# A third place for the half spectrum of a pair in a spectral mixer's forward transform

## The chip, the cores and the metric

One core of one Trainium2 chip runs the whole program. The metric is the device time of one execution in microseconds, as the median of several runs; next to it stands one execution that was taken by the hardware profiler.

## What is computed

The reference is one block of a conditioned network, forward and backward (grad_out comes in, the output and nine gradients go out). Cut to what matters here:

```python
def _A_ref(x, w_r, w_i):                       # S = 2048, D = 1024
    X = jnp.fft.rfft2(x.astype(jnp.float32), axes=(-2, -1))
    X = X * (w_r + 1j * w_i)                   # [2048, 513]
    return jnp.fft.irfft2(X, s=(S, D), axes=(-2, -1)).astype(jnp.bfloat16)

def _B_ref(x, w1, b1, w2, b2):                 # F = 3584
    y = _layernorm(x)
    h = _gelu(y @ w1 + b1)
    return h @ w2 + b2

sa, ca, ga, sb, cb, gb = (silu(c) @ w_mod)     # six rows of 1024
h = _layernorm(x) * (1 + ca) + sa
x = x + ga * _A_ref(h, A_w_r, A_w_i)
h = _layernorm(x) * (1 + cb) + sb
x = x + gb * _B_ref(h, B_w1, B_b1, B_w2, B_b2)
```

The gradients of A_x, A_w_r, A_w_i, B_w1, B_b1, B_w2, B_b2, c and w_mod are computed as well.

## The kernel before, in words

The two-dimensional transform is done with matrix products on folded data. `spectral_core` is called twice: with `fwd=True` for the forward pass and with `fwd=False` for the gradient. Its stages are:

- `s_fwd` transforms along the 2048 tokens, in four classes of rows (CE, SE, CO, SO), with matmuls `pu` that land in the tiles `U`.
- `pair(n, par, m)`, for n = 0 to 7, transforms along the features (matmuls `pcs`, line 505) and casts the results into `cs` (two buffers, `css[n % 2]`). From `cs`, VectorE builds the half spectrum of a pair of row blocks in the tile `Pt`, by a sum and a difference of 128 x 1028 elements. In the forward pass GpSimd stores `Pt` to DRAM as `d_P[n]` (line 523), where the backward pass will read it. Then VectorE multiplies `Pt` by the two weight planes `ws` (products `qa` and `qb`), adds and subtracts them, and writes two rows of `R`.
- `s_inv` transforms back along the tokens (matmuls `pv`, line 565, from `R` to the tiles `V`). The classes CE and SE are done between pair 5 and pair 6, since they need R of pairs 0 to 3; CO and SO are done after pair 7.
- the last loop transforms back along the features (matmuls `po` into `ct`), and `consume` does what follows.

The tiles of a pair come from `new_pair_temps`. `ws2`, `Pt2` and `qa2` hold two places each, used in turn. `qb2` also has two halves: the forward pass uses half 0 for the product `qb`, for every pair, and only the backward pass uses half 1 (product `m2`). The weights of pair n + 1 are fetched by `pair_load`: one plain DMA from SP and one gather from GpSimd for each of the two planes (lines 490 and 491).

Beside the forward transform, TensorE has filler work: `ph_part` (matmuls `pp`, line 684) multiplies the gradient by B_w2 and is laid out over the whole stretch. Later come the two layers of the mixer (lines 802 and 851), their gradients (948, 1071, 1252), and the backward transform with gradient matmuls as filler.

The program is written as a data flow of tiles. A scheduler lays out each engine's order ahead of time, from the dependencies, the order in the text, `tc.high_priority()` (for the casts that empty PSUM) and `tc.issue_after()`; `nc.any` lets it choose the engine of a cast. It also sets the waits: an instruction that writes a buffer waits for those that still read it, DMAs included. Each engine then runs its instructions strictly in the order laid out, and so does GpSimd with the DMAs that it issues.

VectorE's tensor operations go through the helper `tt`, so that the profile shows them all at line 173, and they are told apart by their tiles.

## Time and profile before

| | |
|---|---|
| median of 3 runs | 1469.18 us (1469.07 to 1473.41) |
| the profiled execution | 1474.63 us |
| its span, from the first to the last instruction | 1472.8 us |
| TensorE busy | 1395.1 us, 95% of the span |
| VectorE busy | 1072.9 us, 73% |
| ScalarE busy | 717.8 us, 49% |
| GpSimd busy | 376.5 us, 26% |
| mean granted TensorE clock | 0.988 |
| HBM traffic | 186 GB/s over the span |
| forward pairs, from the first to the last Pt row | 157.6 to 213.8 us |

A time in a row of the profile is the start in us from the first instruction of the span, then the duration. What stands in brackets at the end of a row of the timeline is the idle time of that engine just before it, and what ended it. A row `out<-in` names the tile written and the tiles read; `x8` counts instructions. A row of the waits has the total in us, how often, and the longest. DMA transfers are not rows of the timeline; a row of POOL or SP with DMA in its name is the instruction that issues the transfer.

### The profile page before, as it was taken

The page shows a single profiled execution, that of the slowest core. Times are in us where ns is not written, and L with a number is a line of the kernel's source. Part 1 is how long each engine was busy: PE and PEld are TensorE (multiplying, and loading weights), DVE is VectorE, ACT ScalarE, POOL GpSimd, SP SyncE. Part 2 cuts the span into 40 slices and gives each one's busy share as a digit, 9 for nine tenths or more (in the row PEclk, how much of TensorE's full clock was granted, in tenths as well). Part 3 has the DMA queues.
Part 4 walks back from the last instruction along what each step waited for, and adds up shares of the span by engine and source line. Part 5 has one row for each costly group of instructions (what it writes and reads, how often), then busy time and mean ns, then how long its engine had stood idle before and what let it go on. Part 6 is the DMA issues. An engine that isn't in the chain of part 4 may idle for free. (4 is left out here: it accounts for less than half of the span.)

```text
span 1472.8 us, 18265 instructions
## 1 busy us (share of the span) xinstructions
PE 1395.1 (95%) x6703; PEld 650.6 (44%) x6835; DVE 1072.9 (73%) x1581; ACT 717.8 (49%) x953; POOL 376.5 (26%) x441
## 2 busy tenths in 40 slices
PE   5889989999999999999989999999999999999997
PEld 2434545444444444444434444444444444444443
DVE  5984786898799788887520789888467578898542
ACT  4765545857887666665312333342622434444211
POOL 5720541211112222122211011021245431322422
PEclk9999999999999999999999999999999999999999
DMA  9982563999777776796999275396699998766993
GB/s 335 279 228 58 144 219 114 262 258 335 242 245 232 235 248 223 229 292 216 235 303 250 91 256 186 121 266 172 184 226 242 236 218 220 191 193 181 291 235 115
DMA packets 358366, 324.27 MB, mean 220 GB/s; under 512 B 209386, under 2 KB 301056, under 8 KB 358022
## 3 DMA queue, kind: packets, MB, share of 16 engines
q1 hardware_dynamic: 324166, 207.71, 52.9%
q0 software_dynamic: 34112, 115.41, 22.8%
q8 instruction: 53, 0.87, 0.2%
q14 instruction: 35, 0.29, 0.1%
HBM read 162.06 MB, written 111.20 MB: 186 GB/s over the span
## 5 line engine op out<-in xcount | busy, mean ns | idle before, releaser
L684 PE MATMUL pp<-gBoT,wt 128*128 128x512 bf16 x878 | 196.8, 381 | 5.8 <-DMA wt<-in_B_w_dram 3.2
L948 PE MATMUL pg<-w1T,gzr 128*128 128x512 bf16 x876 | 194.6, 379 | 1.6 <-ACT gn3a L956 0.2
L1252 PE MATMUL gw1acc<-gzh,n3n 128*128 128x512 bf16 x876 | 193.8, 379 | 2.3 <-DMA gzh<-d_gz 1.3
L802 PEld LDWEIGHTS <-w 128*128 128x128 bf16 x896 | 87.6, 98 | 112.5 <-issue 9.0
L684 PEld LDWEIGHTS <-wt 128*128 128x128 bf16 x896 | 87.7, 98 | 109.9 <-issue 4.2
L948 PEld LDWEIGHTS <-gzr 128*128 128x128 bf16 x896 | 86.8, 98 | 107.9 <-issue 4.9
L1252 PEld LDWEIGHTS <-n3n 128*128 128x128 bf16 x896 | 87.5, 98 | 106.1 <-issue 2.8
L802 PE MATMUL pz<-n3Ta,w 128*128 128x512 bf16 x437 | 99.4, 383 | 6.1 <-ACT gt L805 4.1
L1071 PE MATMUL gw2acc<-gB,hhsA 128*128 128x512 bf16 x438 | 99.3, 384 | 3.7 <-ACT gwo L1078 3.1
L802 PE MATMUL pz<-n3Tb,w 128*128 128x512 bf16 x439 | 98.4, 379 | 0.5
L851 PEld LDWEIGHTS <-hhA 128*128 128x128 bf16 x608 | 59.4, 98 | 77.5 <-issue 8.0
L811 ACT ACTIVATE gt<-gt 128x2048 bf16<-128x2048 bf16 x28 | 53.5, 1911 | 71.1 <-DVE gt L173 71.1
L805 ACT ACTIVATE gt<-pz,b_col 128x512 bf16<-128x512 f32 x112 | 72.8, 684 | 28.9 <-PE pz L802 26.9
L173 DVE TENSOR_TENSOR gt<-gt,gt 128x2048 bf16<-128x2048 bf16 x56 | 68.5, 1223 | 21.6 <-ACT gt L813 20.9
L1256 ACT CAST gwo<-gw1acc 128x512 bf16<-128x512 f32 x50 | 29.0, 584 | 113.0 <-PE gw1acc L1252 98.7
L1078 ACT CAST gwo<-gw2acc 128x512 bf16<-128x512 f32 x46 | 26.8, 584 | 111.7 <-PE gw2acc L1071 84.0
L173 DVE TENSOR_TENSOR ct<-ct 128x2048 bf16<-128x2048 bf16 x64 | 75.9, 1217 | 2.6 <-DMA d_n<-ct 1.8
L992 DVE CUSTOM_DVE_ANT_0 otl<-otl 128x1024 bf16<-128x1024 bf16 x24 | 29.0, 1222 | 57.5 <-DMA otl<-in_w_mod_dram 51.5
L1071 PEld LDWEIGHTS <-hhsA 128*128 128x128 bf16 x448 | 44.1, 99 | 56.4 <-DMA hhsA<-d_hh 3.6
L807 ACT ACTIVATE gt<-gt 128x2048 bf16<-128x2048 bf16 x28 | 53.4, 1908 | 0.6
L813 ACT ACTIVATE gt<-gt 128x2048 bf16<-128x2048 bf16 x28 | 53.4, 1907 | 0.5
L1257 POOL DMA_DIRECT2D out_dram<-gwo x56 | 30.9, 553 | 78.9 <-ACT gwo L1256 46.8
(317 smaller groups left out, 2520.1 us busy)
## 6 DMA issues: line engine op xcount, KB each, us to landing
gzr<-d_gz SPq DMA_DIRECT2D x28, 512.0 KB
wblk<-in_w_mod_dram SPq DMA_DIRECT2D x12, 1024.0 KB
out_dram<-otl POOLq DMA_DIRECT2D x48, 256.0 KB
out_dram<-gwo POOLq DMA_DIRECT2D x96, 128.0 KB
d_ph<-pho POOLq DMA_DIRECT2D x21, 512.0 KB
d_hh<-hhA POOLq DMA_DIRECT2D x19, 512.0 KB
w2sD<-in_B_w_dram SPq DMA_DIRECT2D x14, 512.0 KB
hhC<-d_ph SPq DMA_DIRECT2D x14, 512.0 KB
```

The source lines that it names most:

```text
L173: return nc.vector.tensor_tensor(out=out, in0=a, in1=b, op=op)
L684: last_pe[0] = nc.tensor.matmul(pp[:], lhsT=wt[:, fg % 2, cch, k * P:(k + 1) * P], rhs=gBoT[j][:, cch, :], start=(cch == 0), stop=(cch == ...
L802: last_pe[0] = nc.tensor.matmul(pz[:], lhsT=w1s[g][:, cch, k * P:(k + 1) * P], rhs=n3T[:, cch, :], start=(cch == 0), stop=(cch == NDC - 1))
L805: nc.scalar.activation(out=zb[:, k, :], in_=pz[:], func=ACT.Identity, bias=b1_col[:, fc:fc + 1], scale=1.0)
L807: nc.scalar.activation(out=av, in_=zb, func=ACT.Square)
L811: nc.scalar.activation(out=sg, in_=bv, func=ACT.Sigmoid, scale=2.0 * GK)
L813: nc.scalar.activation(out=bv, in_=bv, func=ACT.Sigmoid, scale=-2.0 * GK)
L851: last_pe[0] = nc.tensor.matmul(pbs[i][:], lhsT=hh[:, k, i * P:(i + 1) * P], rhs=wp[:, k, :], start=False, stop=(g == 6 and k == 3))
L948: last_pg[0] = nc.tensor.matmul(pgs[i][:], lhsT=gzs[b, g][:, k, i * P:(i + 1) * P], rhs=w1Ts[g][:, k, h * KH:(h + 1) * KH], start=(g == 0 ...
L1071: nc.tensor.matmul(acc[:], lhsT=hh_of(fc)[:, t, :], rhs=gBs[t // 4][:, t % 4, h * KH:(h + 1) * KH], start=(t == 0), stop=(t == NT - 1))
L1252: nc.tensor.matmul(acc[:], lhsT=n3ns[t // 4][:, t % 4, cch * P:(cch + 1) * P], rhs=gz2[t // 8][:, t % 8, :], start=(t == 0), stop=(t == NT ...
L1257: nc.gpsimd.dma_start(out=out_4[cch * P:(cch + 1) * P, fg * 512:(fg + 1) * 512], in_=ob)
```

## The change

In the forward pass the place of `Pt` now goes round three instead of two. Pairs 0, 3 and 6 use place 0 of `Pt2`, pairs 1, 4 and 7 place 1, and pairs 2 and 5 use half 1 of `qb2`, seen in the shape of a place of `Pt2`. The backward pass keeps its two places. Nothing else is touched: the stores to `d_P`, the products and their order in the text are the same.

```diff
@@ pair, in spectral_core @@
-            Pt = Pt2[:, n % 2]
+            Pt = qb2[:, 1].rearrange("p a b w -> p (a b) w") if fwd and n % 3 == 2 else Pt2[:, n % 3 if fwd else n % 2]
             cv = cs.rearrange("p t (x w) -> p t x w", w=PW)
             tt(Pt[:, 2:0:-1, :], cv[:, 0], cv[:, 1], ALU.add)
             tt(Pt[:, 0:4:3, :], cv[:, 0], cv[:, 1], ALU.subtract)
```

## The prediction

> **What bounds the kernel now.** The page comes first. TensorE is busy for 95% of the span, so a change pays only where it fills an idle stretch of TensorE, or where it raises its clock.

> ```profile
> span 1472.8 us, 18265 instructions
> ...
> PE 1395.1 (95%) x6703; PEld 650.6 (44%) x6835; DVE 1072.9 (73%) x1581; ACT 717.8 (49%) x953; POOL 376.5 (26%) x441
> ```

> Next, the view of who waited for whom, between 100 and 420 us, first for TensorE and then for VectorE. The edited lines run here, from 154 to 220 us.

> ```profile
> PE pv L565 <- DVE R L173: 3.9, 1, 3.9
> ...
> DVE Pt L173 <- DMA d_P<-Pt: 2.5, 1, 2.5
> ```

> VectorE waits once for the buffer that the change adds. TensorE waits once for R. The timeline shows that they are one chain:

> ```profile
> 181.31 0.58 POOL L523 DMA_DIRECT2D d_P<-Pt  x1
> ...
> 188.72 0.69 DVE L173 TENSOR_TENSOR Pt<-cs 128x1028 bf16<-128x1028 bf16 x1 [2.47 <-DMA d_P<-Pt]
> ...
> 191.14 1.29 DVE L173 TENSOR_TENSOR R<-qa 128x1026 bf16<-128x1026 bf16 x2
> ...
> 191.89 1.03 PE L565 MATMUL pv<-smi,R 128*128 128x512 bf16 x2 [3.93 <-DVE R L173]
> ...
> 198.89 0.69 DVE L647 CAST V<-pv 128x512 bf16<-128x512 f32 x1 [1.15 <-PE pv L565]
> ```

> Counting the 16 Pt rows from 157.61 us, those at 188.72 and 190.54 are pair 4. Its place is pair 2's, and pair 2's store was issued only at 181.31, because two gathers held GpSimd (rows below). The sums for pair 4 stand in VectorE's order ahead of the last four steps of pair 3 (two on qa, two on R), so R of pair 3 is late. TensorE has used up its filler (pp in the timeline, from 182.94 to 187.95) and stands for 3.94 us. The stretches show what the clock does then (time; PE, PEld, DVE, ACT and POOL busy; granted clock; DMA share, GB/s):

> ```profile
> 191.00:192.00 1.00, 0.11 (x1) 0.11 (x2) 1.00 (x3) 0.68 (x2) 0.48 (x1) 0.88 0.88 353
> 192.00:193.00 1.00, 1.00 (x4) 0.39 (x4) 1.00 (x2) 1.00 (x3) 0.10 (x1) 0.50 0.43 173
> ...
> 195.00:196.00 1.00, 1.00 (x6) 0.40 (x5) 1.00 (x3) 0.56 (x1) 1.00 (x1) 0.91 0.53 134
> ```

> From 191.76 to 195.18, 3.42 us, the clock is half: 1.71 us of work lost.

> **The change part by part.** No instruction is added or removed. Pt of pairs 2 and 5 goes to the idle half of qb2, and the other pairs alternate so that a place is reused after three pairs.

> *Pair 4's wait, removed.* Pair 4 now takes pair 1's place, whose store was issued at 165.24; the longest store seen took 7.41 us from issue (181.31 to 188.72), so it is free by 172.7. The other conditions hold: cs of pair 4 was cast from 172.81 to 174.75. The sum starts at 186.25 behind qb: 2.47 us earlier. R of pair 3 ends at 189.36 instead of 191.83 and TensorE resumes at 189.42: **-2.47 us**.

> *The half clock, removed.* The gap left is 3.94 - 2.47 = 1.47 us. A gap of 2.07 us ahead of 1291.18 leaves the clock at 1.00, so this one should: **-1.71 us**. By then TensorE is 4.18 us ahead.

> *What is late next.* The seventh tile of V is cast by VectorE, between the two R steps of pair 4 (198.89). TensorE would have it ready at 194.65 (198.83 - 4.18) and the next one, in the other PSUM place, 0.86 us later at 195.51. VectorE's first R step ended at 197.74; shifted by 2.47 that is 195.27, and the cast (0.69) frees the place at 195.96, some 0.05 more with the signal. TensorE gives back **+0.50 us**. All that follows hangs on TensorE (cs of pair 6 at 207.18, ct at 234.04, where VectorE had been idle 11.9 us), and moves by the same amount.

> *Reuse of the third place and the others*, **0**: pair 5 wants its place at 192.16, whose store landed at 188.72. Pairs 6 and 7 want theirs after 205; their stores were issued at 186.09 and 191.52, and with 7.41 us are in by 198.9. Cover for pair 5 is 3.4 us; without it the sum would wait for the remainder.

> *Time of the sums and products*, **0**: the places are 4,112 bytes long and lie alike; the same sums take 681 ns in the forward tiles and 688 ns in the backward ones.

> *ws of pair 4*, **0**: its products are wanted at 189.88 and 191.02. GpSimd ended its gathers at 184.26 and 185.51. The one gather that VectorE waited for (pair 3's second, 1.61 us) ended at 181.31 and released qb at 185.01, 3.70 us later; that gives 187.96 and 189.21. The bounds are 0 and 2.47, since at 192.35 nothing was waited for; I take the end nearest to the 3.70 row.

> *ws of pair 5* is what I am least sure of. Its gathers ran in VectorE's pause, which the change closes:

> ```profile
> 169.44 4.75 POOL L491 DMA_INDIRECT ws<-in_A_w_r_dram,xu  x1 [3.63 <-DVE qa L173]
> ...
> 175.08 6.23 POOL L491 DMA_INDIRECT ws<-in_A_w_i_dram,xu  x1 [0.30 <-issue]
> ...
> 186.97 1.02 POOL L491 DMA_INDIRECT ws<-in_A_w_r_dram,xu  x1 [0.30 <-issue]
> ```

> The third had the pause; the first two had two-input work on VectorE with no break, and ended 0.93 us after VectorE turned to a cast from PSUM (173.26, 180.37). Yet those at 161.65 and 163.72, beside the same kind of work, took 1.76 and 1.48. Between a cost of 0 and of 1.6 us (second rival) I take 0, because products of pair 5 come 9 us after the issue.

> [...]

> **Sum:** -2.47 - 1.71 + 0.50 = -3.7 us. The profiled execution took 1474.63 (span 1472.8 and 1.83 around it), so it would be 1470.9. That execution lies 5.45 above the median 1469.18 of the runs; taken off the median, 1465.5, which is 0.25%. The bound of 0.3%, about what a measurement of this kernel can tell from no change, is 4.4 us.

> **The rivals.**

> 1. *Forecast*, 1465.5. Its own spread is the clock's: a gap of 3.08 us (ahead of 1132.86) brought half clock, one of 3.18 (ahead of 333.72) none, so gaps of about 3 us can fall either way once all behind 190 has moved. Each is worth 1.7 us: 1463.8 or 1467.2. Two that cost now can fall away (1132.86, and 1206.20 with 3.43), one can appear; so slightly more than half of this case lies beyond -4.4. Chance 0.49: 0.26 faster, 0.23 within.
> 2. *The gain is taken back by ws of pair 5, or was not there to take.* If the gather of 186.97 is held until the cast at 195.27, it ends at 196.20, the second at 197.5, landing at 201.2; from there pair 5 needs 3.89 us (201.24 to 205.13) and ends at 205.1, when cs of pair 6 is wanted at 203.5. The gain shrinks by 1.6, to 2.1: 1467.1. With pairs 6 and 7 pushed back too, 1469.2. The same 1469.2 comes out if the unprofiled runs had no such wait: two of them lie 4.3 us below the third, about the 4.2 of this wait and its clock. Chance 0.15, within.
> 3. *The order is written anew.* The scheduler lays out every engine's order from the dependencies. Seven more pp matmuls (0.223 each, 22 in 4.91) ahead of the wait for R would close the 1.47 us: 1464.0. All 32 of them behind it would leave TensorE idle from 182.94 to 189.42, 6.5 us instead of 3.9, with the half clock: 1471.7, and more where casts change engines. Against it: pairs 1 to 5 stand in one pattern on VectorE (qb, one sum of the next pair, two steps, the other sum, R), so the store did not shape the order of pair 4. Chance 0.21: 0.11 faster, 0.02 within, 0.08 slower.
> 4. *Slower: the store of the third place holds qb.* The third place lies in the tile that every pair's qb writes. If the tile is guarded whole, qb of pair 2 (176.21) waits for pair 2's store to land: at 180.1 if it is issued as soon as the sums end (172.73 + 7.41), at 188.72 if it stays behind both gathers. The hold is 3.9 to 12.5 us, the middle 8.2. Pair 4's wait is gone but R of pair 3 comes 8.2 - 2.47 = 5.7 later, and TensorE stands for it: 1474.9. It decides from a hold of 6.9 us (2.47 + 4.4). Against it: pair 3 wrote one half of Pt2 at 177.35 while the store of the other half was issued only at 181.31, so halves are guarded apart. Chance 0.15: 0.12 slower, 0.03 within.

> **How the numbers follow.** Faster 0.26 + 0.11 = 0.37; slower 0.08 + 0.12 = 0.20; within 0.23 + 0.15 + 0.02 + 0.03 = 0.43. The likeliest single case has 1465.5, with its own range 1463.8 to 1467.2. The range for 8 in 10 holds it, the second rival, and the inner parts of the third and fourth: 1461 to 1473. Left out are the upper half of the fourth and the ends of the third.

> **What the changed profile would show.** Right: no Pt waiting for d_P; TensorE's wait for R down from 3.9 to about 1.5 us; clock 1.00 throughout 187 to 197; the V cast on VectorE directly behind R. The second rival: a POOL gather near 187 that takes 5 to 9 us, and qa or qb of pair 5 waiting for ws. The third: another number of pp matmuls ahead of pv near 190. The fourth: qb waiting for d_P. The forecast is wrong if the wait for d_P is gone and TensorE's stand near 190 is not shorter.

## The result, and the profile after

| | before | after |
|---|---|---|
| median of the runs | 1471.55 us (22 runs; the first three of them gave the 1469.18 of above) | 1465.61 us (22 runs) |
| lowest and highest | 1466.2 and 1478.5 | 1461.02 and 1470.12 |
| the profiled execution | 1474.63 us | 1469.58 us |
| its span | 1472.8 us | 1467.6 us |
| forward pairs and the first half of `s_inv` (see below) | 79.34 us | 75.32 us |

The ratio is 0.9961, with a 95% interval of 0.9948 to 0.9974: faster by 0.39%, or 5.7 us (3.8 to 7.7). The middle of the interval lies beyond the bound of 0.3%, its lower end (0.26%) just inside.

The page first. The instructions are the same in number, and TensorE's share of the span is as before.

```profile
span 1467.6 us, 18265 instructions
...
PE 1397.0 (95%) x6703; PEld 652.8 (44%) x6835; DVE 1073.8 (73%) x1581; ACT 718.0 (49%) x953; POOL 365.7 (25%) x441
```

Who waited for whom, of TensorE and VectorE, between 150 and 215 us (total, how often, the longest):

```profile
DVE qb L173 <- DMA ws<-in_A_w_i_dram,xu: 1.4, 1, 1.4
...
PE pv L565 <- DVE R L173: 1.1, 1, 1.1
...
PE pv L565 <- ACT V L647: 0.2, 1, 0.2
```

There is no row in which VectorE waits for `d_P`. TensorE's wait for R is down from 3.9 to 1.1 us. The timeline of the same spot, after:

```profile
180.56 0.59 POOL L523 DMA_DIRECT2D d_P<-qb  x1
...
184.04 1.23 DVE L173 TENSOR_TENSOR qb<-Pt,ws 128x2052 bf16<-128x2052 bf16 x1 [1.38 <-DMA ws<-in_A_w_i_dram,xu]
...
185.19 0.69 DVE L173 TENSOR_TENSOR Pt<-cs 128x1028 bf16<-128x1028 bf16 x1
...
187.60 1.29 DVE L173 TENSOR_TENSOR R<-qa 128x1026 bf16<-128x1026 bf16 x2
...
188.35 0.61 PE L565 MATMUL pv<-smi,R 128*128 128x512 bf16 x2 [1.14 <-DVE R L173]
...
193.51 0.69 DVE L173 TENSOR_TENSOR R<-qa 128x1026 bf16<-128x1026 bf16 x1
194.12 0.69 DVE L647 CAST V<-pv 128x512 bf16<-128x512 f32 x1
```

The store of pair 2 now reads `qb` (half 1 of `qb2`) and is issued as late as before, still behind both gathers. But pair 4's sum at 185.19 follows `qb` without a bracket, so it waits for nothing. The clock (time; PE, PEld, DVE, ACT and POOL busy; granted clock; DMA share, GB/s) stays at 1.00 in every microsecond from 186 to 197; three of them:

```profile
187.00:188.00 1.00, 0.21 (x1) 0.00 (x0) 1.00 (x3) 0.23 (x1) 0.70 (x2) 1.00 0.89 283
188.00:189.00 1.00, 0.65 (x4) 0.41 (x5) 1.00 (x3) 1.00 (x3) 1.00 (x1) 1.00 1.02 397
...
191.00:192.00 1.00, 1.00 (x7) 0.41 (x5) 1.00 (x3) 0.72 (x2) 1.00 (x1) 1.00 0.89 247
```

**A measure of the stage.** The 22 runs of before spread over 12 us, so differences of 2 us are read from a stretch of the trace instead: from the first `pcs` matmul of pair 0 to the long row of `po` matmuls behind the last pair. The two rows that begin it and end it, in the timeline of before:

```profile
154.50 5.52 PE L505 MATMUL pcs<-em,U 128*128 128x256 bf16 x48
...
233.84 8.46 PE L630 MATMUL po<-gm,V 128*128 128x256 bf16 x76
```

and of after:

```profile
153.76 5.51 PE L505 MATMUL pcs<-em,U 128*128 128x256 bf16 x48
...
229.08 8.46 PE L630 MATMUL po<-gm,V 128*128 128x256 bf16 x76
```

233.84 - 154.50 = 79.34 and 229.08 - 153.76 = 75.32, so the stage lost 4.02 us. A second profiled execution of the changed kernel (e11 below) gave 75.34. This measure is called "the stage" from here on. One run of e4 below, 1843 us, was slow and is left out of its ratio; all others are fast.

### The profile page after: what moved, and what is told of

Same layout as the page of the kernel before. It is cut to its first block, busy times and chain, and to the rows that moved or that the text cites. A ratio compares the mean times of both kernels' runs of the same rounds, so it can differ in the third digit from the quotient of the medians.

```text
span 1467.6 us, 18265 instructions
## 1 busy us (share of the span) xinstructions
PE 1397.0 (95%) x6703; PEld 652.8 (44%) x6835; DVE 1073.8 (73%) x1581; ACT 718.0 (49%) x953; POOL 365.7 (25%) x441
## 5 line engine op out<-in xcount | busy, mean ns | idle before, releaser
L173 DVE TENSOR_TENSOR gt<-gt,gt 128x2048 bf16<-128x2048 bf16 x56 | 68.5, 1224 | 21.6 <-ACT gt L813 20.9
L173 DVE TENSOR_TENSOR ct<-ct 128x2048 bf16<-128x2048 bf16 x64 | 75.9, 1218 | 2.0 <-DMA d_n<-ct 1.2
```

Of the source, the lines that this page charges most:

```text
L173: return nc.vector.tensor_tensor(out=out, in0=a, in1=b, op=op)
```

## The experiments

The theory was the prediction's: pair 2's store is late only because two gathers of weights hold GpSimd, pair 4 has to wait for it because it shares its place, TensorE then stands with no filler, and a stand of 3.9 us brings half clock. The rivals were that one of the two re-used places does all of it, that the DMA itself (and not its place in GpSimd's queue) is slow, and that the gathers of later pairs take the gain back.

All kernels below keep the orders of TensorE, VectorE and ScalarE of before; only places, issuing queues and GpSimd's order differ. Stage and time:

| | places | pair 2's store | stage, us | ratio to before (95%) |
|---|---|---|---|---|
| before | 2 | behind two gathers | 79.34 | |
| after | 3 | behind two gathers | 75.32 | 0.9961 (0.9948 to 0.9974) |
| after, again (e11) | 3 | behind two gathers | 75.34 | 0.9948 (0.9932 to 0.9964) |
| e1 | third for pair 4 | behind two gathers | 76.71 | 0.9994 (0.9977 to 1.0011) |
| e2 | third for pair 5 | behind two gathers | 79.02 | 0.9992 (0.9977 to 1.0006) |
| e3 | 2 | between the gathers | 74.81 | 0.9968 (0.9948 to 0.9989) |
| e4 | 2 | behind four gathers | 81.12 | 1.0013 (0.9999 to 1.0027) |
| e5 | 3 | behind four gathers | 74.67 | 0.9960 (0.9941 to 0.9978) |
| e6 | 2 | no gathers | 73.81 | 0.9986 (0.9966 to 1.0007) |
| e7 | 3 | no gathers | 73.83 | 0.9985 (0.9970 to 1.0001) |
| e8 | 3 | from SP | 74.29 | 0.9973 (0.9957 to 0.9988) |
| e10 | 2 | from SP | 74.96 | 0.9973 (0.9947 to 0.9999) |
| e9 | 3 | between the gathers | 74.97 | 0.9935 (0.9916 to 0.9954) |
| e9 again (e12) | 3 | between the gathers | 75.27 | 0.9971 (0.9954 to 0.9988) |

**The third place for pair 4 alone, and for pair 5 alone.** Against before, one line each (e1 and then e2):

```diff
-            Pt = Pt2[:, n % 2]
+            Pt = qb2[:, 1].rearrange("p a b w -> p (a b) w") if fwd and n == 4 else Pt2[:, n % 2]
```

```diff
-            Pt = Pt2[:, n % 2]
+            Pt = qb2[:, 1].rearrange("p a b w -> p (a b) w") if fwd and n == 5 else Pt2[:, n % 2]
```

> Two places as before, but the forward pass puts pair 4 alone into the idle half of the second product's tile. Theory W (all of the gain comes from pair 4's wait for pair 2's store, with the half clock behind it): the wait of Pt for d_P is gone, TensorE's wait for R is 1 to 1.5 us instead of 3.9, no half clock between 187 and 197, and the kernel is as fast as with three places, 4 us (0.27%) under before on TensorE's own order, within the noise of the runs. Rival P (the other pairs' longer reuse matters too): less than half of the gain, under 2 us.

> Two places as before, but the forward pass puts pair 5 alone into the idle half of the second product's tile; pair 4 still shares pair 2's place. Theory W: the wait of Pt for d_P stays (2 to 3 us), TensorE's wait for R stays near 3.9 us with half clock behind it, and the time is that of before (within 0.1%). Rival P: part of the gain, 1 to 3 us.

With pair 4 moved, its wait is gone and TensorE's stand for R is 1.27 us. But the stage gains only 2.63 us, not 4.0, since pair 5 now waits for pair 3's store. The timeline of e1:

```profile
187.92 0.61 PE L565 MATMUL pv<-smi,R 128*128 128x512 bf16 x2 [1.27 <-DVE R L173]
...
191.94 0.71 DVE L173 TENSOR_TENSOR Pt<-cs 128x1028 bf16<-128x1028 bf16 x1 [1.18 <-DMA d_P<-Pt]
...
195.71 7.07 PE L565 MATMUL pv<-smi,R 128*128 128x512 bf16 x32 [1.19 <-DVE V L647]
```

The wait of 1.18 us delays the cast of the seventh V tile, which stands on VectorE behind pair 5's two sums and a step of R of pair 4, and TensorE stands 1.19 us for it. So the expectation that pair 4's move alone would be as fast as three places fell, though the gain is more than rival P's 2 us: the rotation over three also serves pair 5, and that is worth 76.71 - 75.32 = 1.4 us. In the runs e1 is not told from before.

With pair 5 moved (the control), the wait of pair 4 is 2.52 us, the stand 3.89 us, and the clock is half from 191.48 to 194.90 (worked out from the granted clock of each microsecond): the chain of before, and a stage within 0.32 us of it.

**The store's place in GpSimd's queue.** Two kernels keep two places. In e3 the store of pair 2 is issued between the two gathers of pair 3's weights (and each later store likewise); in e4 it is issued behind the gathers of pair 4's.

```diff
-                nc.gpsimd.indirect_dma_start(out=ws[:, x, 1, 0:DF], out_offset=None, in_=w, in_offset=w_idx(par, m))
+                with tc.issue_after(r_in[1].ins) if fwd and n > 1 and x == 1 else ExitStack(): nc.gpsimd.indirect_dma_start(out=ws[:, x, 1, 0:DF], out_offset=None, in_=w, in_offset=w_idx(par, m))
...
-                nc.gpsimd.dma_start(out=d_P[n], in_=Pt.rearrange("p a w -> p (a w)"))
+                r_in[1:] = [nc.gpsimd.dma_start(out=d_P[n], in_=Pt.rearrange("p a w -> p (a w)"))]
```

> Two places as before; only GpSimd's order differs: in the forward pass the second gather of a pair's weights is issued behind the store of the pair before. Theory W (the store is late because two gathers hold GpSimd): pair 2's store is issued near 175 instead of 181.3 and lands by 183, so pair 4 does not wait although it shares pair 2's place; the gain is that of three places, about 4 us, less what a gather that comes 1 us later costs at pair 3's product (its wait for ws grows from 1.6 to at most 2.6 us). Rival D (the store is slow in the DMA engines, not late on GpSimd): the wait for d_P stays above 1.5 us and the time is that of before.

```diff
-                nc.gpsimd.indirect_dma_start(out=ws[:, x, 1, 0:DF], out_offset=None, in_=w, in_offset=w_idx(par, m))
+                g = nc.gpsimd.indirect_dma_start(out=ws[:, x, 1, 0:DF], out_offset=None, in_=w, in_offset=w_idx(par, m))
+                if fwd and (n, x) == (4, 1):
+                    with tc.issue_after(g.ins):
+                        nc.gpsimd.dma_start(out=d_P[2], in_=late[0].rearrange("p a w -> p (a w)"))
...
-            if fwd:
-                nc.gpsimd.dma_start(out=d_P[n], in_=Pt.rearrange("p a w -> p (a w)"))
+            if fwd and n == 2: late[:] = [Pt]
+            elif fwd: nc.gpsimd.dma_start(out=d_P[n], in_=Pt.rearrange("p a w -> p (a w)"))
```

> Two places as before, but pair 2's store is issued behind both gathers of pair 4's weights, near 185.5 instead of 181.3. Theory W: pair 4's wait grows by about as much, from 2.5 to 5 to 7 us, TensorE's wait for R grows from 3.9 to 6.5 to 8.5 us, the half clock lasts one or two windows of 3.4 us, and the kernel is 2.5 to 5 us (0.2 to 0.35%) slower than before. Rival H (TensorE's stand is made up later, beside the VectorE-bound stage): same time as before within 0.1%.

The timeline of e3, with two places:

```profile
174.17 0.59 POOL L523 DMA_DIRECT2D d_P<-Pt  x1
...
183.49 1.23 DVE L173 TENSOR_TENSOR qb<-Pt,ws 128x2052 bf16<-128x2052 bf16 x1 [0.69 <-DMA ws<-in_A_w_i_dram,xu]
...
187.80 0.61 PE L565 MATMUL pv<-smi,R 128*128 128x512 bf16 x2 [0.44 <-DVE R L173]
```

Issued 20.26 us into the stage, 6.55 us earlier than in before (26.81), the store makes nobody wait, and the stage is 4.53 us shorter than before. The wait came from the store's place in the queue. VectorE's wait for ws of pair 3, expected to grow to at most 2.6 us, fell to 0.69 instead.

And e4 (the edit shifts the lines: the store is L492):

```profile
185.22 0.58 POOL L492 DMA_DIRECT2D d_P<-Pt  x1
...
188.87 0.70 DVE L173 TENSOR_TENSOR Pt<-cs 128x1028 bf16<-128x1028 bf16 x1 [4.48 <-DMA d_P<-Pt]
...
192.04 1.03 PE L565 MATMUL pv<-smi,R 128*128 128x512 bf16 x2 [5.17 <-DVE R L173]
```

Counted from the start of the stage, the store is issued 5.0 us later than in before (31.80 against 26.81) but lands only 1.23 us later (35.45 against 34.22), 3.65 us after its issue and not 7.41. TensorE stands 1.24 us longer, 5.17 instead of 3.93. VectorE's wait is 4.48 us, not the 5 to 7 expected; the rest of its 2 us over before is only that it is ready for the sum 0.78 us earlier. The clock is half for two windows (from 189.72 to 196.54) instead of one; the part of them that lies in the stand, up to 192.04, costs nothing, so by the granted clock they cost 0.5 x 4.50 = 2.25 us against 1.65 in before. Together that is +1.24 + 0.60 = 1.84, and the stage is 1.78 us longer. The direction holds in the stage, though the loss is under the 2.5 us expected. The time, +0.13% (-0.01 to +0.27), does not tell e4 from before, nor theory W from rival H.

**The late store with three places.** e4's edit on the changed kernel. The expectations of e5 to e8 count the stage from the first store's issue to the first gather of `xt`; by that count before took 47.05 us, the changed kernel 43.03, e5 44.39, e6 and e7 41.55 each, and e8 42.27.

> Three places, with pair 2's store issued behind both gathers of pair 4's weights as in the run before. From the first store's issue to the first gather of xt the stage took 47.05 us before, 43.03 with three places, and 48.88 with two places and the late store. Theory W (a third place lets the store be late at no cost): pair 5 wants its place near 191 and the store lands near 189, so no wait for d_P, a stage of 42.5 to 43.5 us, 4 us (0.27%) under before. Rival: pair 5 waits in place of pair 4, as it did for pair 3's store when pair 4 alone had been moved; a stage of 44 to 46.

The late store costs nothing there: no wait for `d_P`, a stage of 74.67 us from `pcs` to `po`. By the expectation's own count e5 missed, but not for the rival's reason: GpSimd came late to the gather of `xt`, since its last gather of weights began only at 202.97. This run also shows the second rival at work, which the other traces of the changed kernel do not (its gathers are at L489):

```profile
188.07 7.02 POOL L489 DMA_INDIRECT ws<-in_A_w_r_dram,xu  x1 [0.30 <-issue]
...
197.37 1.23 DVE L173 TENSOR_TENSOR qa<-qb,ws 128x2052 bf16<-128x2052 bf16 x1 [1.95 <-issue]
```

A gather of pair 5's weights took 7.02 us, and VectorE stood 1.95 us ahead of pair 5's `qa` (the profile names no cause; that it waited for these weights is inferred from the two rows). It cost the stage nothing: TensorE has the CE and SE classes to do at that time, and in the changed kernel VectorE has 2.04 us to spare behind R of pair 5 (it ends at 200.37, the next cast starts at 202.41).

**No gathers at all.** In the forward pass SP fetches both planes with plain DMAs (e6 with two places, e7 with three; R, V and what follows from them are computed with other weights for the mirrored rows).

```diff
-                nc.gpsimd.indirect_dma_start(out=ws[:, x, 1, 0:DF], out_offset=None, in_=w, in_offset=w_idx(par, m))
+                nc.sync.dma_start(out=ws[:, x, 1, 0:DF], in_=w_plus(w, par, m)) if fwd else nc.gpsimd.indirect_dma_start(out=ws[:, x, 1, 0:DF], out_offset=None, in_=w, in_offset=w_idx(par, m))
```

> Two places; in the forward pass the mirrored weight rows are not gathered by GpSimd, but loaded by SP with the plain load's rows, so that the weights of the mirrored half are other ones. Theory G (GpSimd's gathers, held beside VectorE's two-input work, make the store late): pair 2's store is issued by 174, nobody waits for d_P or ws, TensorE's wait for R is under 1.5 us, and the stage takes 41.5 to 43 us instead of 47.05; 4 to 5.5 us faster in all. Rival D (the DMA engines are slow at that point): a wait for d_P of over 1 us stays, stage 45 us or more.

> As the run before, with three places. Theory G: where no gather holds GpSimd the third place is worth nothing: the stage differs by less than 0.3 us from that with two places. Rival (a third place helps by itself): at least 1 us shorter.

Pair 2's store in e6, and in e7:

```profile
172.39 0.53 POOL L523 DMA_DIRECT2D d_P<-Pt  x1 [2.02 <-DVE Pt L173]
```

```profile
172.15 0.53 POOL L523 DMA_DIRECT2D d_P<-qb  x1 [2.02 <-DVE qb L173]
```

GpSimd now idles for the sums, not the sums for GpSimd. The stage is the shortest of all, and the third place is worth 73.83 - 73.81 = nothing. So what the change removes is only what the gathers cause.

**The store from SP.** One line, on the changed kernel (e8) and on before (e10):

```diff
-                nc.gpsimd.dma_start(out=d_P[n], in_=Pt.rearrange("p a w -> p (a w)"))
+                nc.sync.dma_start(out=d_P[n], in_=Pt.rearrange("p a w -> p (a w)"))
```

> Three places, and the store to d_P is issued by SP instead of GpSimd; tried for a faster version. Theory G: GpSimd's gathers lose a store between them and start up to 0.9 us earlier, so VectorE's wait for ws of pair 3 (1.4 us) and TensorE's for R (1.1) shrink by up to 0.9 each: a stage of 42 to 43 us. Rival S: SP stands for Pt's sums and the plain weight loads and transposes queued behind the store come later; stage 43 to 46, no better than three places.

> Two places as before, with the store to d_P issued by SP. Theory W: the store of pair 2 does not stand behind gathers, pair 4 does not wait, and the stage is that of three places with this store, 74.3 us, within 0.4. Rival S: SP reaches the store late (it stands for the weight loads and transposes) and pair 4 waits 1 us or more; stage 76 us or more.

With two places SP's store does what the third place does: no wait for `d_P`, and 74.96 us, although 0.67 us over e8 and not within the 0.4 expected. With both the stage is 74.29, 1.03 us under the changed kernel, as theory G of e8 had it: VectorE's wait for ws of pair 3 and TensorE's for R are gone. Neither is faster than the changed kernel in the runs.

**Order and third place together, and the changed kernel again.** e9 and e12 are one kernel: e3's edit on the changed kernel. e11 is the changed kernel, unedited.

> Three places together with the order in which pair 2's store goes ahead of the second gather; tried for a faster version. The stage from the first pcs matmul to the long run of po matmuls took 79.34 us before, 75.32 with three places, 74.81 with two places and this order. Theory W (both remove the same wait): the two gains do not add, the stage is 74.3 to 74.9 us. Rival: they add, 71 to 73 us.

> The changed kernel once more, beside the next run on one chip. Theory W (all of the gain lies in the stage, 4.0 us): 0.2 to 0.35% under before, a stage of 75.2 to 75.5 us. Rival X (something behind the stage gains as well): 0.4% or more under before, with the time from the start of the po run to the end at least 1.5 us shorter than before's 1239.0.

> Three places with the store ahead of the second gather, once more: the first time gave 0.65% under before from few runs, with a stage only 4.4 us (0.30%) shorter. Theory W: that was the scatter behind the stage; this time 0.2 to 0.45%, within 0.15% of the changed kernel on the same chip. Rival X: again 0.5% or more, so that this order gains some 4 us outside the stage.

The gains of the early store and of the third place do not add: 74.97 and 75.27 against 75.32 with the third place alone. e9's ratio of 0.9935 rests on six runs, and that of the repeat, 0.9971, has an interval that overlaps the changed kernel's (e11, same chip), though the two are 0.23% apart and not 0.15. e11 itself met both signs of rival X: 0.52% under before, and from the stage's end to the end of the span 1235.8 us against 1239.0. In e12 VectorE waits 0.82 us for ws of pair 4 and TensorE 0.81 us for the V cast behind it, so what the early store wins is given back there. No version beat the changed kernel by more than two takes of one kernel differ.

**What hides differences of 2 us.** In the traces the clock's loss (1 minus the granted clock, summed over time) can be set beside the length of what lies behind the stage:

| | lost to the clock behind 240 us | from the stage's end to the end of the span |
|---|---|---|
| before | 9.1 | 1239.0 |
| after | 11.0 | 1238.5 |
| e1 | 13.0 | 1241.1 |
| e3 | 5.2 | 1231.5 |
| e4 | 4.9 | 1231.2 |
| e11 | 7.3 | 1235.8 |

Over all 14 traces (two of the changed kernel, two of e9's) the two columns go together with a correlation of 0.93 and 1.1 us of length for 1 us lost; the length varies by 10 us, and with the loss taken off by 4. The program behind the stage is the same in all of them. So the traces differ there above all by the number of half-clock windows, two to six of 1.7 us each beside what is lost at the very end. Ahead of 150 us the loss varies too (5.1 to 11.9 us), but there it costs nothing: the stage starts between 153.20 and 154.97 whatever was lost (correlation 0.03). That the runs scatter for the same reason is likely but not shown. A run has only the mean clock of its whole span on record: over the 104 runs of before listed below its loss goes with the time at a correlation of 0.54, and taking it off does not narrow the scatter (a standard deviation of 3.1 us with it, 3.3 without).

**Where the rest of the runs' gain is.** The stage lost 4.0 us, the runs 5.7 and (e11) 7.7. The runs give a mean granted clock as well, so the loss, (1 - clock) x span, can be averaged over them (us; the error of a mean is 0.3 to 0.5 in the first two lines and about 1 in the others):

| | mean time | lost to the clock | remainder |
|---|---|---|---|
| before (104 runs beside e1 to e12) | 1472.7 | 20.8 | 1451.9 |
| after (22 runs and the 10 of e11) | 1465.1 | 16.8 | 1448.3 |
| e1 | 1472.4 | 20.0 | 1452.5 |
| e3 | 1466.4 | 16.8 | 1449.6 |
| e6 | 1470.8 | 20.8 | 1450.0 |
| e7 | 1470.2 | 20.9 | 1449.3 |

The changed kernel loses 4.0 us less to the clock on average. If every run of before has the stage's window, that is 1.7 of it; the other 2.3 are some 1.4 windows fewer per run elsewhere. That is near the size of the surplus, but it does not show the cause. A mean does not tell where the windows lie, and those ahead of 150 us cost nothing. The remainder fell by 3.6 us, of which the stage without its window explains only 2.3. And the profiled pair itself shows one window more behind the stage after than before (11.0 and 9.1 us). e6 and e7 have the shortest stage and the same mean loss as before, so they have some more windows elsewhere; that accounts for about half of the 3 us or more by which their stage's 5.5 us is missing from their time, and the rest is open. Why a changed stage should leave more or fewer windows far behind it stays open: none of the kernels varied that alone.

## Why the prediction was right

The time, 1465.5, met the median of 1465.61, but that is luck, since two misses of the same size cancel in it: the median that it was taken off, 1469.18 of three runs, lay 2.4 us below that of 22 runs, and the medians differ by 5.9 instead of 3.7 us. In the stage, where the steps can be checked, the forecast of 3.7 stands against 4.02. Followed matmul by matmul on TensorE, the gain is 2.80 + 1.50 - 0.27 = 4.03: from the stand, from the clock, and given back. The prediction's sum had 2.47 + 1.71 - 0.50.

*Pair 4's wait, removed.* Right. The wait is gone because the place was taken from a store still in the queue (e3 removes it with two places, e4 lengthens it). The stand for R was forecast at 1.47 us and was 1.14. Of the difference 0.23 is VectorE's wait for ws of pair 3, 1.38 instead of 1.61, which the sum left as it was; the rest, 0.1, is that pair 4's sum starts 0.08 us before the end of `qb`, where the sum of the prediction put it behind that end.

*The half clock, removed.* Right: 1.00 throughout 186 to 197. The term was a little large, 1.50 instead of 1.71: it counted the whole window, though TensorE still stood in the first 0.13 us of it. The stands of the runs order it: 1.14 and 1.27 us no window, 3.89 and 3.93 one, 5.17 two. The one window of before is 3.42 us long (191.76 to 195.18), the two of e4 are 6.82 together (189.72 to 196.54). Length alone does not order all stands, though: in the changed kernel a stand of 2.70 us ahead of 328.47 brought one, while in before a stand of 3.18 ahead of 333.72 brought none. In the traces it depends on how a stand falls on the windows (last section). With one exception, in e11, half clock followed no full-clock window (14 traces, 150 to 1450 us) in which TensorE was busy for more than 0.43 of 3.41 us. Taken from that share, one stand would have to take some 1.9 us (0.57 x 3.41, an estimate) out of a window in which TensorE is otherwise busy, and 1.14 or 1.47 does not reach that wherever it falls; the 2.07 us ahead of 1291.18, on which the prediction relied, were split by a boundary at 1290.86.

*Given back, +0.50.* This term was wrong. The V cast does stand directly behind R on VectorE, as forecast, but TensorE lost nothing there. VectorE's first R step ended 2.80 us earlier, not 2.47, and TensorE came with the tile 4.03 us ahead, not 4.18; so the cast ended at 194.81, just before the next tile was ready (194.06 + 0.86 = 194.92). What TensorE did give back, 0.27 us, it gave earlier, ahead of 189.61, where it waited 0.21 us for ScalarE's cast of V; the half clock had hidden that wait in before. The cast on VectorE came at 194.12, 40.36 us from the start of the stage; in before it came at 198.89, which is 44.39. So at this point 4.03 us had been won, and the forecast had 3.7.

*Reuse of the third place and the others, 0.* Right, for the reason given: pair 5 finds the third place free. e1 shows what this zero rests on, 1.4 us if pair 5 stays on pair 3's place.

*ws of pair 4 and of pair 5, 0.* Right in the traces of the changed kernel: pair 5's gathers took 1.15 and 1.48 us although VectorE no longer paused. In e5 the 7.02 us gather of the second rival did appear and cost the stage nothing, but not by the cover that was named: `qa` of pair 5 came 9.3 us after the gather's issue and VectorE still stood 1.95 us. What covered it were VectorE's 2.04 us to spare behind R of pair 5; the rival's price of 1.6 us came from a delay of pair 5 by some 3.7 us, which no trace shows. The rival held the gather until VectorE turned to a cast. The 7.02 us gather agrees with that: it ended at 195.09, 0.97 us after the start of the V cast in the changed kernel's trace (194.12; the row of `pv` ahead of it starts at 189.61 in both traces). The two of 1.15 and 1.48 us beside two-input VectorE work do not.

*The rivals.* The third and the fourth did not occur: every engine's order is the same as before, and no `qb` waits for `d_P`. The doubt in the second rival, that unprofiled runs lack the wait, has nothing left to rest on: the runs gain 3.8 to 7.7 us, where the trace's stage lost 4.02.

*The forecast's own spread.* It put 1.7 us on each clock window that appears or falls away. That was the right unit, but it looked for them near stands of about 3 us alone; stands of 2.22 (ahead of 1199.46) and 2.70 us brought one in the changed kernel too, and one of 3.18 us in before brought none. On average over the runs some 1.4 windows fell away beside the one in the stage.

## What to carry to other kernels

Before a buffer is added, look at what makes it late: here GpSimd issued a store of 4,112 bytes per partition only at 181.31, behind two gathers of 4.75 and 6.23 us, and issuing it earlier, issuing it from another queue, or a third place each removed some 4 to 4.5 us of the stage, and the third place joined with either of the other two gave 4.1 to 5.1, not the sum. When a place is added, rotate over all users: moving only the one that waited left the next pair waiting (1.18 us in e1). And when gains of a few us do not show in the time, read the stage in the trace, and sum the clock's loss over the part behind it; the mean clock of a whole run does not tell where the loss lies.

## What the runs showed of the hardware that was not expected

```profile
326.03:329.44 3.41, 0.97 (x5) 0.50 (x6) 3.41 (x5) 3.41 (x4) 0.00 (x0) 1.00 1.33 276
329.44:332.85 3.41, 3.41 (x10) 1.22 (x9) 3.41 (x3) 1.46 (x3) 1.30 (x2) 0.50 0.92 171
```

- The stand of 3.18 us is longer, but split by a boundary at 331.71: it leaves 0.66 and 0.41, and the clock stays full (before):

```profile
328.29:331.71 3.42, 2.25 (x11) 0.81 (x9) 3.42 (x6) 1.79 (x4) 0.00 (x0) 1.00 0.86 318
331.71:335.12 3.41, 1.40 (x7) 0.70 (x8) 3.41 (x6) 3.41 (x5) 0.00 (x0) 1.00 1.22 221
335.12:338.53 3.41, 3.41 (x18) 1.52 (x17) 3.41 (x4) 1.71 (x4) 1.30 (x2) 1.00 1.03 237
```

- A store of this size, issued from GpSimd, took 7.41 us to land when issued at 181.31 (before) and 3.65 when issued at 185.22 (e4), both read from the end of VectorE's wait. Moving it also shortened a neighbour: with the store away from 181 us, VectorE's wait for ws of pair 3 fell from between 1.3 and 1.6 us (before, after, e1, e2, e11) to between 0.5 and 0.8 (e3, e4, e5, e9, e12).
- Gathers of one shape held GpSimd for 0.95 to 7.02 us, plain DMA issues beside the forward pairs for 0.53 to 0.60. The long ones (4.75 and 6.23 us in before, 7.02 in e5) have two-input VectorE work beside them; why some beside the same work are short (1.15 and 1.48 us in the changed kernel) was not isolated.
